# Threshold attention ahead of a two-layer network: transposed weights in the scores' spare PSUM columns, a new order of a period's instructions, and a small add moved to GpSimd

## The chip, the cores and the metric

The kernel runs on one core of a Trainium2 chip. The metric is the device time of one execution in microseconds (us); the lower the better. The core has five engines that matter here: TensorE (PE in the profile, with its weight loads as PEld), VectorE (DVE), ScalarE (ACT), GpSimd (POOL), and SyncE (SP), which issues the transfers. Each engine works through its own list of instructions in order, and waits at an instruction until the semaphores named in it have come.

## The reference, cut to what matters

```python
batch, n_heads, seq, head_dim = (8, 8, 576, 64)          # q, k, v: fp32
scores = (1 / sqrt(64)) * matmul(q, k.T)                 # per head: 576 x 576
thresh = max(scores, axis=-1) - tau                      # tau = 0.02
scores = where(scores >= thresh, scores, -1e9)
attn = exp(scores - max(scores))
attn = attn / (sum(attn) + 1e-9)
x = matmul(attn, v)  ->  (4608, 512)                     # heads side by side
h = maximum(x @ w_in, 0)                                 # w_in (512, 2048)
out = (h * h) @ w_out                                    # w_out (2048, 512)
```

The softmax has a threshold: of each row only the scores within tau of the row's maximum keep a weight, and the row is then divided by its sum plus 1e-9.

## The kernel before

The program has two stages. The attention comes first. The two layers of the network follow it, as products of blocks with sums of blocks formed ahead and after (a scheme that takes 49 block products where a plain one takes 64). The change touches only the attention.

Heads are taken two at a time: 32 pairs. The 576 query rows of a pair are four blocks of 128 and a rest of 64; the rests of two pairs make one more block. So there are 144 units of 128 rows by two heads, and `period(p)` handles two at once, A = 2p and B = 2p+1, over 72 periods, with a few more at both ends to fill and drain. The order of instructions is written out by hand in `period`: the order of the calls is the order on every engine, and the framework only adds the waits between engines.

The work of a unit, and where it runs:

- `scores_rest` (L373, or L376 for a shared rest) and `scores` (L386), on TensorE, write the scores of both heads into one tile `sc` of three PSUM banks, 1536 columns. Head 0 takes columns 0 to 575, head 1 takes 960 to 1535; columns 576 to 959, all in the middle bank, are spare (`SPARE`). There are two `sc` tiles, which fill six of the eight PSUM banks.
- `top` (L401, VectorE) finds the negative row maxima of both heads, `least` (L404, VectorE) the thresholds, `power` (L409, ScalarE) the exponentials of one head, `mask` (L414, VectorE) zeroes what lies under the threshold and sums the rows, `over` (L420, VectorE) adds 1e-9 to the two sums, `inverse` (L423, VectorE) takes reciprocals, and `normal` (L426, GpSimd) multiplies one head's weights by them.
- `fill` (L454, TensorE) transposes the weights, 9 blocks of 128x128 a unit and 18 for the two units of a period, into PSUM, and `filled` (L461, ScalarE) copies them to a tile `wT` in SBUF. These transposes go to the two PSUM banks that `bank` hands out in turn (`pY`), and six go into the two `pv` banks, behind the results there.
- `values` (L472, TensorE) multiplies them by v, two periods after the scores. Its results in the two `pv` banks are copied out together with the first six transposes of the next pair of units, and go to DRAM as x.

`turn` (L336, copied out in L339 or L341) transposes the queries or the keys of the next pair; `turn_last` (L351) does the rest of both, with its copies in L355 and L356 and two small GpSimd copies in L359. A table `TURNS` says which periods do it: of nine, four turn queries, four turn keys and one turns nothing.

The weights of the network are prepared beside the attention: `convert1` to `convert6` (L203 and L210 on ScalarE, L217 and L241 on GpSimd, L225 and L233 on VectorE) convert one of 32 pieces from 64-bit to 32-bit floats in each of 32 periods, and `sums_step` makes one of the 88 sums of weight blocks on GpSimd (L132 and L135), up to three in a period that converts nothing.

SyncE issues all loads and stores in one queue: queries (L291), keys (L305, L309), the rests (L310), values (L320), x (L518), weights (L183) and the finished weight sums (L521).

Of the kernel before, what the change touches and what calls it, by code (L numbers as in the profile page):

```python
# [48 lines left out]
def kernel(  # L49
# [236 lines left out]
    def load_q(i):  # L286
        b, hp = pairs[i]
        h = 2 * hp
        qn = sb.tile([P, FULL, P], FP32, tag="qn", name="qn")
        for j in range(2):  # L290
            nc.sync.dma_start(  # L291
                out=qn[:, :, ds(j * D, D)], in_=q[b, h + j, 0:MAIN, :].rearrange("(t p) d -> p t d", p=P)
            )
        loaded[i] = [qn]

    def load_k(i):
        b, hp = pairs[i]
        h = 2 * hp
        kn = sb.tile([P, FULL, P], FP32, tag="kn", name="kn")
        rn = sb.tile([P, P], FP32, tag="rn", name="rn")  # L300
        for j in range(2):
            queue = nc.scalar if i == 0 and j == 0 else nc.sync
            keys = k[b, h + j, :, :].rearrange("(p c) d -> p c d", c=CH)
            for e in range(2):
                queue.dma_start(  # L305
                    out=kn[ds(e * HALF, HALF), :, ds(j * D, D)],
                    in_=keys[:, j : j + CH - 1, :].rearrange("p (t e) d -> p t e d", e=2)[:, :, e, :],
                )
            queue.dma_start(out=rn[REST:P, ds(j * D, D)], in_=keys[:, 0 if j else CH - 1, :])  # L309
        nc.sync.dma_start(  # L310
            out=rn[0:REST, :].rearrange("p (j d) -> p j d", j=2),
            in_=q[b, h : h + 2, MAIN:S, :].rearrange("j p d -> p j d"),
        )
        loaded[i] += [kn, rn]

    def load_v(i):
        b, hp = pairs[i]
# [5 lines left out]
        )  # L323
        loaded_v[i] = va

    def turn(i, which):

        if which == 0:
            turned[i] = (
                sb.tile([P, MAIN], FP32, tag="qT", bufs=2, name="qT"),  # L330
                sb.tile([P, S], FP32, tag="kT", bufs=3, name="kT"),
            )
        nat, to = loaded[i][which], turned[i][which]
        pt = bank([P, FULL, P], "pqk")
        for t in range(FULL):
            nc.tensor.transpose(pt[:, t, :], nat[:, t, :], ident[:, :])  # L336
        flat, to = pt[:, :, :].rearrange("p t m -> p (t m)"), to[:, 0:MAIN]
        if which:
            nc.scalar.copy(to, flat)  # L339
        else:  # L340
            nc.scalar.activation(out=to, in_=flat, func=AF.Identity, scale=qscale[:, :])  # L341
            if i + 1 < len(pairs):
                load_q(i + 1)

    def last_q(i):
        return qdiag[i // 2 % 2][:, i % 2, :]

    def turn_last(i, pt):

        rn = loaded.pop(i)[2]  # L350
        nc.tensor.transpose(pt, rn[:, :], ident[:, :])  # L351

        def then():
            to = last_q(i)[:, ds(i % 2 * REST, REST)]
            nc.scalar.activation(out=to, in_=pt[:, 0:REST], func=AF.Identity, scale=qscale[:, :])  # L355
            nc.scalar.copy(turned[i][1][:, MAIN:S], pt[:, REST:P])  # L356
            for j in range(2):
                rows = ds(j * D, D)
                nc.gpsimd.tensor_copy(out=kdiag[i % 3][rows, ds(j * REST, REST)], in_=turned[i][1][rows, MAIN:S])  # L359
            if i + 1 < len(pairs):  # L360
                load_k(i + 1)

        return then

# [2 lines left out]
    def scores_rest(n, sc):  # L367
# [7 lines left out]
        for c, i in enumerate(pair):  # L375
            nc.tensor.matmul(to, last_q(i)[:, :], kdiag[i % 3][:, :], start=(c == 0), stop=(c == 1))  # L376

    def scores(n, sc):

        pair, t = units[n]  # L380
        for c in range(2):
            for j in range(2):
                rows, at = ds(j * D, D), ds(c * HALF, HALF)
                qT, kT = turned[pair[c]]
                lhs = qT[rows, ds(t * P + c * HALF, HALF)] if t < FULL else last_q(pair[c])[rows, at]
                nc.tensor.matmul(sc[at, ds(j * 2 * BANK, MAIN)], lhs, kT[rows, 0:MAIN], start=True, stop=True)  # L386

    AT = (0, 2 * BANK - REST)

    def softmax(n, sc):  # L390
# [26 lines left out]
            )  # L417

        def over():
            nc.vector.tensor_scalar(out=sm, in0=sm, scalar1=1e-9, scalar2=None, op0=ALU.add)  # L420

        def inverse():
            nc.vector.reciprocal(out=rs, in_=sm)  # L423
# [8 lines left out]
    def do(n, what, *args):  # L432
# [2 lines left out]

    wT = {}

    FILLS = (
        [(0, c) for c in range(3)], [(1, c) for c in range(3)],
        [(0, c) for c in range(3, 7)], [(1, c) for c in range(3, 7)],  # L440
        [(u, c) for c in (7, 8) for u in range(2)],
    )
    AT_OF = {
        uc: f * BANK + (P * (i + 1) if f < 2 else P * i) for f, fill in enumerate(FILLS) for i, uc in enumerate(fill)
    }

    def fill(m, f, pt):

        if has(2 * m):
            if m not in wT:  # L450
                wT[m] = sb.tile([P, 5 * BANK], FP32, tag="wT", bufs=1, name="wT")
            for i, (u, c) in enumerate(FILLS[f]):
                w = weights[2 * m + u]
                nc.tensor.transpose(pt[:, ds(P * (i + (f < 2)), P)], w[:, c, :, :].rearrange("p j d -> p (j d)"), ident[:, :])  # L454
        else:
            wT[m] = sb.tile([P, 5 * BANK], FP32, tag="wT", bufs=1, name="wT")

    def filled(m, f, pt, pv=False, copy=nc.scalar.copy):

        a, z = P if f < 2 and not pv else 0, BANK if has(2 * m) else P  # L460
        copy(wT[m][:, ds(f * BANK + a, z - a)], pt[:, a:z])  # L461

    def values(m):

# [2 lines left out]
        for c in range(CH):  # L467
            for u in range(2):
                for s, (i, _, count, row) in enumerate(halves(2 * m + u)):
                    for j in range(2):  # L470
                        rows = ds(j * D, D)
                        nc.tensor.matmul(  # L472
                            out[j][ds(u * D, D), ds(row, count)], loaded_v[i][rows, c, :],
                            x[rows, ds(AT_OF[u, c] + row, count)],
                            start=(c == 0 and s == 0), stop=(c == CH - 1), skip_group_check=True,
                        )
        return out
# [9 lines left out]
                    if i + 3 < len(pairs):  # L487
                        load_v(i + 3)

    def give_x(m, x):  # L490

        for u in range(2):
            rows = ds(u * D, D)
            for i, first, count, row in halves(2 * m + u):
                b, hp = pairs[i]
                to = xT[b][ds(hp * P, P), ds(first, count)].rearrange("(j d) n -> d j n", j=2)
                of = x[rows, 0 : 2 * BANK].rearrange("p (j n) -> p j n", j=2)[:, :, ds(row, count)]
                given.append((to, of))

    def has(n):  # L500
        return 0 <= n < NU
# [27 lines left out]
    def begun(n):  # L529
        return starts.get(n)  # L530

    TURNS = {}
    for g in range(2, 2 * len(pairs)):
        two, x = divmod(g - 4, 4)
        TURNS.setdefault(max(1, (9 * two + 5 + 2 * x) // 2), []).append(g)

    def period(p):

        A, B_, a, b = 2 * p, 2 * p + 1, 2 * p - 2, 2 * p - 1
# [13 lines left out]
                return pt  # L553

        def begin(n):
            if has(n):
                sc[n] = sc_pool.tile([P, 3 * BANK], FP32, tag="sc", name="sc")
                scores_rest(n, sc[n])

        do(a, "mask", 0)  # L560
        do(a, "mask", 1)
        do(a, "over")
        do(a, "inverse")
        do(a, "normal", 0)
        do(a, "normal", 1)
        begin(A)
        if has(A):
            scores(A, sc[A])
            softmax(A, sc[A])
        convert3(begun(p - 1))  # L570
        pt4 = other(m, 4)
        if pt4:
            filled(m, 4, pt4)
        for g in turns:
            turn(g // 2, g % 2)
        convert1(begun(p))
        convert2(begun(p))
        then = None
        begin(B_)
        if turns and turns[-1] % 2:  # L580
            then = turn_last(turns[-1] // 2, sc[B_][:, SPARE : SPARE + P])
        do(b, "mask", 0)
        do(b, "mask", 1)
        if has(B_):
            scores(B_, sc[B_])
            softmax(B_, sc[B_])
        do(A, "top")
        do(b, "over")
        do(b, "inverse")
        do(b, "normal", 0)  # L590
        do(b, "normal", 1)
        pv = values(m) if has(2 * m) else None
        do(A, "power", 0)
        do(A, "least")
        do(A, "power", 1)
        do(B_, "top")
        if then:
            then()
        pt0 = first(0, pv)
        pt1 = first(1, pv)  # L600
        do(B_, "power", 0)
        if pt0:
            filled(m + 1, 0, pt0, pv)
        if pt1:
            filled(m + 1, 1, pt1, pv)
        if pv:
            valued(m)
            give_x(m, wT[m + 1])
        do(B_, "power", 1)
        ask(False)  # L610
        convert4(begun(p - 1))
        do(B_, "least")
        convert5(begun(p - 1))
        sums_step()
        pt2 = other(m + 1, 2)
        if pt2:
            filled(m + 1, 2, pt2)
        pt3 = other(m + 1, 3)
        if pt3:
            filled(m + 1, 3, pt3)  # L620
        convert6(begun(p - 1))
        sums_start(p)
        if begun(p - 1) is None:
            sums_step()
        if begun(p - 1) is None:
            sums_step()
        fetch(begun(p + 2))
        ask(False)
# [304 lines left out]
    with tc.manual_schedule():  # L933
        with ExitStack() as stack:
# [15 lines left out]
            nc.scalar.activation(out=first[:, 0, :], in_=ident[:, 0:2], func=AF.Exp)  # L950
            load_v(0)
            keep_busy(10)
            turn(0, 0)
            turn(0, 1)
            turn_last(0, bank([P, P], "pqkr")[:, :])()
            for i in range(1, 3):
                load_v(i)
# [126 lines left out]
```

## Time and profile before

| | |
|---|---|
| three runs, median | 1408.46 us (1407.82 to 1408.79) |
| the profiled execution, its own time | 1406.65 us |
| its span, first to last instruction | 1404.9 us |
| clock of TensorE granted | 0.998 of full speed |
| first and last maximum (L401) | 12.0 and 591.0 us |
| first product of the two layers in the chain that ended last | 606.17 us |
| PE, DVE, ACT, POOL busy over the whole span | 96%, 76%, 61%, 67% |

The profile is one execution of the program. A row of the groups by line names the line of the kernel, the engine, the operation, the tiles written and read, the shapes and the count; then the total busy time in us and the mean of one in ns; then the idle time of that engine just before these instructions, and what ended most of it. A row of the timeline begins with the start in us and the duration of the merged instructions in us. Matmuls overlap and their ends are modelled, so TensorE's steps are best read from one start to the next. Nearly all tiles of the attention lie in one big tile, which the profile calls `arena`.

### The profile page before, as it was taken

The numbers are of one execution on the slowest core, as the hardware profiler recorded it, in microseconds if no ns is written. First come the engines' busy times: TensorE is split into PE (matmuls) and PEld (weight loads), VectorE is DVE, ScalarE is ACT, GpSimd is POOL, SyncE is SP. The second block draws the span as 40 slices with busy tenths as digits, with TensorE's granted clock in tenths as the row PEclk, the third lists the DMA queues.
The fourth block names the chain that finished last, engine by engine and source line by source line (L and its number), as shares of the span: only waits on it lengthen the run. The fifth ranks groups of instructions, "written<-read, shape, count | busy, mean of one in ns | idle before, by whom it ended". The sixth has DMA issues, their size and how long they took to land.

```text
span 1404.9 us, 40543 instructions
## 1 busy us (share of the span) xinstructions
PE 1351.1 (96%) x15882; PEld 1188.3 (85%) x15882; DVE 1070.6 (76%) x2280; ACT 850.6 (61%) x1579; POOL 943.8 (67%) x967
## 2 busy tenths in 40 slices
PE   7999999899999999999999999999999999999998
PEld 4676666666666767699999999999999999999998
DVE  5999999999999998857787778877765456654563
ACT  5888777688887777737665667656643233332330
POOL 2666788867778885335665566555887777777775
PEclk9999999999999999999999999999999999999999
DMA  4554326785432222123323433237962444224411
GB/s 113 130 138 129 81 56 187 208 262 156 123 100 64 72 64 68 29 69 131 114 105 111 144 128 113 103 110 282 396 208 87 147 150 144 67 96 147 151 32 31
DMA packets 205295, 177.24 MB, mean 126 GB/s; under 512 B 96304, under 2 KB 149552, under 8 KB 205104
## 3 DMA queue, kind: packets, MB, share of 16 engines
q1 hardware_dynamic: 203792, 174.24, 40.2%
q8 instruction: 125, 2.05, 0.6%
q14 instruction: 66, 0.54, 0.1%
q10 hardware_dynamic: 1312, 0.41, 0.1%
HBM read 105.12 MB, written 69.47 MB: 124 GB/s over the span
## 4 chain that ended last, share of the span: by engine, by line
PE 53%; DVE 1%; POOL 1%; ACT 1%; issue 0%; DMA 0%; DVEq 0%; POOLq 0%
PE po L891 28%; PE ph L756 25%; DVE arena L135 1%; POOL arena L135 1%; ACT arena L670 0%; ACT arena L735 0%; DMA w<-w 0%; DVEq L135 0%; POOLq L135 0%; ACT arena L736 0%
## 5 line engine op out<-in xcount | busy, mean ns | idle before, releaser
L135 POOL TENSOR_TENSOR arena<-arena 128x512 f32<-128x512 f32 (+1 forms) x314 | 376.4, 1220 | 252.4 <-DVE arena L135 213.7
L756 PE MATMUL ph<-arena,w 128*128 128x128 f32 x3528 | 396.6, 275 | 1.9 <-DVE arena L135 0.8
L756 PEld LDWEIGHTS ph<-arena,w 128*128 128x128 f32 x3528 | 394.7, 192 | 3.8 <-DVE arena L135 3.1
L891 PE MATMUL po<-w,arena 128*128 128x128 f32 x3528 | 396.6, 275 | 0.3
L891 PEld LDWEIGHTS po<-w,arena 128*128 128x128 f32 x3528 | 394.8, 192 | 2.0 <-issue 1.6
L135 DVE TENSOR_TENSOR arena<-ph,arena 128x512 f32<-128x512 f32 x378 | 255.7, 689 | 94.1 <-PE ph L756 63.4
L426 POOL TENSOR_SCALAR arena<-arena 128x576 f32<-128x576 f32 x288 | 211.2, 747 | 130.3 <-DVE arena L404 65.0
L135 DVE TENSOR_TENSOR arena<-po,arena 128x128 f32<-128x128 f32 x378 | 108.2, 290 | 169.4 <-PE po L891 165.8
L414 DVE SCALAR_TENSOR_TENSOR arena<-sc,arena 128x576 f32<-128x576 f32 x288 | 222.9, 811 | 11.8 <-ACT arena L409 11.2
L409 ACT ACTIVATE arena<-sc,arena 128x576 f32<-128x576 f32 x288 | 206.4, 752 | 28.1 <-DVE arena L401 20.4
L401 DVE TENSOR_REDUCE arena<-sc 128x2 f32<-128x1152 f32 x144 | 195.2, 1355 | 26.7 <-PE sc L386 25.9
L702 ACT COPY c<-arena 128x512 f32<-128x512 f32 (+1 forms) x303 | 172.9, 579 | 63.0 <-DVE arena L132 55.8
L472 PEld LDWEIGHTS pv<-arena 64*64 64x64 f32 x5760 | 154.9, 133 | 36.9 <-issue 21.6
L454 PEld LDWEIGHTS pY<-ident,arena 128*128 128x128 f32 x864 | 90.4, 140 | 112.6 <-ACT arena L461 104.4
L132 DVE TENSOR_TENSOR arena<-arena,c 128x512 f32<-128x512 f32 (+1 forms) x267 | 175.0, 664 | 7.8 <-ACT c L702 6.9
L132 POOL TENSOR_TENSOR arena<-arena 128x512 f32<-128x512 f32 (+1 forms) x138 | 174.3, 1263 | 9.7
L461 ACT COPY arena<-pY 128x512 f32<-128x512 f32 x216 | 120.7, 604 | 79.8 <-PE pY L454 79.8
L454 PE MATMUL pY<-ident,arena 128*128 128x128 f32 x864 | 129.9, 286 | 32.9 <-ACT arena L461 32.9
L386 PE MATMUL sc<-arena 64*64 64x512 f32 x1152 | 159.4, 624 | 0.0
L472 PE MATMUL pv<-arena 64*64 64x128 f32 (+1 forms) x5760 | 157.8, 259 | 0.7 <-ACT arena L461 0.7
L735 ACT ACTIVATE arena<-arena 128x512 f32<-128x512 f32 x144 | 89.9, 624 | 77.2 <-POOL arena L135 77.0
L670 ACT COPY arena<-po 128x128 f32<-128x128 f32 x63 | 16.7, 265 | 178.9 <-PE po L891 177.1
(56 smaller groups left out, 1047.2 us busy)
## 6 DMA issues: line engine op xcount, KB each, us to landing
g<-arena SPq DMA_DIRECT2D x144, 256.0 KB, 2.0
arena<-g SPq DMA_DIRECT2D x144, 256.0 KB, 4.7
w<-w SPq DMA_DIRECT2D x98, 256.0 KB, 5.1
arena<-in_v_dram SPq DMA_DIRECT2D x32, 288.0 KB, 3.3
out_dram<-arena SPq DMA_DIRECT2D x70, 128.0 KB, 2.2
arena<-in_q_dram SPq DMA_DIRECT2D x64, 128.0 KB, 3.3
arena<-in_moe_w_out_dram SPq DMA_DIRECT2D x16, 512.0 KB, 4.0
xT<-arena SPq DMA_DIRECT2D x128, 64.0 KB, 2.1
```

The source lines that it names most:

```text
L132: e.tensor_tensor(out=out, in0=x, in1=y, op=ALU.subtract)
L135: e.tensor_tensor(out=out, in0=x, in1=y, op=ALU.add)
L386: nc.tensor.matmul(sc[at, ds(j * 2 * BANK, MAIN)], lhs, kT[rows, 0:MAIN], start=True, stop=True)
L401: nc.vector.tensor_reduce(out=nmx, in_=both, axis=AXIS.X, op=ALU.max, negate=True)
L409: nc.scalar.activation(out=w[:, :, j, :], in_=of(j), func=AF.Exp, bias=nmx[:, j : j + 1], scale=1.0)
L414: nc.vector.scalar_tensor_tensor(out=w[:, :, j, :], in0=of(j), scalar=thr[:, j : j + 1], in1=w[:, :, j, :], op0=ALU.is_ge, op1=ALU.mult, a ...
L426: nc.gpsimd.tensor_scalar(out=w[:, :, j, :], in0=w[:, :, j, :], scalar1=rs[:, j : j + 1], scalar2=1.0, op0=ALU.mult, op1=ALU.mult)
L454: nc.tensor.transpose(pt[:, ds(P * (i + (f < 2)), P)], w[:, c, :, :].rearrange("p j d -> p (j d)"), ident[:, :])
L472: nc.tensor.matmul(out[j][ds(u * D, D), ds(row, count)], loaded_v[i][rows, c, :], x[rows, ds(AT_OF[u, c] + row, count)], start=(c == 0 and ...
L702: nc.scalar.copy(c, y)
L756: nc.tensor.matmul(to[:, j, :], W_IN[m, k][:, ts(j, P)], of[k][:, m - 1, :], start=(not more and j == 0), stop=True, skip_group_check=True,)
L891: nc.tensor.matmul(to, g[:, j, :], w[:, j, :], start=(not more and j == 0), stop=(j == 3), skip_group_check=True)
```

## The change

The 18 transposes of a period are divided anew, in six portions of 1, 3, 3, 4, 4 and 3 (in periods that turn keys 2, 3, 3, 4, 3 and 3). The first two go into the `pv` banks as before, two go into `pY` banks, and the other two, six transposes, go into the spare columns of the `sc` tiles of A and B, between `scores_rest` and `scores`. `apart` tells the framework that the copies of the spare columns and the main scores touch different banks, so that neither has to wait for the other. The tile of the last turn moves from the spare columns to the end of a `pY` bank.

The order in `period` is new. The masks of A now follow in the same period, so `over`, `inverse` and `normal` of A come half a period later than its masks; the masks of B stay at the start of the next period. `over` runs on GpSimd. The steps of the weight conversion and the weight sums are placed anew, and in periods that turn keys and convert nothing, two sums are made in place of three. Keys are loaded as soon as both the keys and the rests of the pair before have been transposed.

```diff
+        def then():
+            if which:
+                nc.scalar.copy(to, flat)
+                next_keys(i)
...
         def over():
-            nc.vector.tensor_scalar(out=sm, in0=sm, scalar1=1e-9, scalar2=None, op0=ALU.add)
+            nc.gpsimd.tensor_scalar(out=sm, in0=sm, scalar1=1e-9, scalar2=None, op0=ALU.add)
...
+            sizes = (2, 3, 3, 4, 3, 3) if turned_last(m + 2) else (1, 3, 3, 4, 4, 3)
+            order = [(u, c) for u in range(2) for c in range(CH)]
...
+        def spare(m, f, n):
+            if has(2 * m):
+                pt = sc[n][:, SPARE : SPARE + 3 * P]
+                fill(m, f, pt)
+                return pt
+
+        pt3 = other(m, 4)
+        then = None
+        if turned_last(p):
+            at = pt3 if pt3 else bank([P, BANK], "pL")
+            then = turn_last(turns[-1] // 2, at[:, 3 * P : 4 * P])
         begin(A)
+        do(b, "mask", 0)
+        convert3(begun(p - 1))
+        do(b, "mask", 1)
+        ptA = spare(m, 2, A)
         if has(A):
             scores(A, sc[A])
             softmax(A, sc[A])
+        if pt3:
+            filled(m, 4, pt3)
+        if then:
+            then()
+        last = [turn(g // 2, g % 2) for g in turns]
+        if ptA is not None:
+            aside(A, filled(m, 2, ptA))
         convert1(begun(p))
+        pt2 = other(m, 3)
+        do(a, "inverse")
+        do(b, "over")
+        do(A, "top")
+        convert4(begun(p - 1))
         begin(B_)
+        ptB = spare(m, 5, B_)
+        do(a, "normal", 1)
+        for done in last:
+            done()
+        if pt2:
+            filled(m, 3, pt2)
+        do(A, "least")
+        if ptB is not None:
+            aside(B_, filled(m, 5, ptB))
+        do(A, "power", 0)
+        do(a, "normal", 0)
         if has(B_):
             scores(B_, sc[B_])
             softmax(B_, sc[B_])
         do(b, "inverse")
+        do(B_, "top")
+        do(A, "power", 1)
+        do(A, "mask", 0)
+        do(A, "mask", 1)
+        convert2(begun(p))
         pv = values(m) if has(2 * m) else None
+        do(b, "normal", 1)
+        do(B_, "least")
         pt0 = first(0, pv)
         pt1 = first(1, pv)
+        do(b, "normal", 0)
         do(B_, "power", 0)
+        sums_step()
         if pt0:
             filled(m + 1, 0, pt0, pv)
+        convert5(begun(p - 1))
+        do(A, "over")
+        do(B_, "power", 1)
         if pt1:
             filled(m + 1, 1, pt1, pv)
...
-        if begun(p - 1) is None:
+        if begun(p - 1) is None and not turned_last(p):
             sums_step()
```

## The prediction

> **What bounds the kernel now.** I read the page first, for the shares, and then the busy time by stretch, because the page averages an attention stage (to about 606 us) with the two layers behind it, which the change does not touch. Columns: start:end, length, then busy us and instructions of each engine, the clock, the DMA share and rate.
>
> ```profile
> 50.00:100.00 50.00, 47.49 (x776) 34.07 (x776) 46.71 (x115) 43.19 (x81) 31.17 (x45) 1.00 0.48 123
> 300.00:350.00 50.00, 46.87 (x728) 32.73 (x721) 49.15 (x109) 42.03 (x78) 36.86 (x48) 1.00 0.66 185
> 500.00:550.00 50.00, 47.49 (x775) 34.11 (x775) 45.23 (x101) 37.24 (x67) 36.61 (x44) 1.00 0.29 73
> ```
>
> TensorE and VectorE are both near full, so the shares alone do not name the bound. The groups by line do better: what each engine idled for.
>
> ```profile
> L454 PEld LDWEIGHTS pY<-ident,arena 128*128 128x128 f32 x864 | 90.4, 140 | 112.6 <-ACT arena L461 104.4
> L454 PE MATMUL pY<-ident,arena 128*128 128x128 f32 x864 | 129.9, 286 | 32.9 <-ACT arena L461 32.9
> L461 ACT COPY arena<-pY 128x512 f32<-128x512 f32 x216 | 120.7, 604 | 79.8 <-PE pY L454 79.8
> L414 DVE SCALAR_TENSOR_TENSOR arena<-sc,arena 128x576 f32<-128x576 f32 x288 | 222.9, 811 | 11.8 <-ACT arena L409 11.2
> L420 DVE TENSOR_SCALAR arena<-arena 128x2 f32<-128x2 f32 x144 | 55.4, 385 | 2.5
> L426 POOL TENSOR_SCALAR arena<-arena 128x576 f32<-128x576 f32 x288 | 211.2, 747 | 130.3 <-DVE arena L404 65.0
> ```
>
> TensorE's transposes into `pY` wait for ScalarE to copy the previous bank out, and ScalarE waits for those transposes: two banks handed to and fro. VectorE spends 55 us on 144 adds of 128x2. The timeline of one period shows both (TensorE's rows, two copies, one add):
>
> ```profile
> 302.31 1.15 PE L454 MATMUL pY<-ident,arena 128*128 128x128 f32 x8 [0.39 <-ACT arena L461]
> 303.10 1.27 POOL L132 TENSOR_TENSOR arena<-arena 128x512 f32<-128x512 f32 x1
> 303.14 1.25 DVE L420 TENSOR_SCALAR arena<-arena 128x2 f32<-128x2 f32 x1
> 303.30 0.42 PE L373 MATMUL sc<-arena 128*128 128x128 f32 x2
> 303.64 1.09 PE L386 MATMUL sc<-arena 64*64 64x512 f32 x8
> 304.67 0.66 PE L454 MATMUL pY<-ident,arena 128*128 128x128 f32 x4
> 305.16 0.60 PE L336 MATMUL pqk<-ident,arena 128*128 128x128 f32 x4
> 306.11 0.49 PE L373 MATMUL sc<-arena 128*128 128x128 f32 x2 [0.36 <-DVE arena L414]
> 306.53 1.09 PE L386 MATMUL sc<-arena 64*64 64x512 f32 x8
> 307.44 2.15 PE L472 MATMUL pv<-arena 64*64 64x128 f32 x72
> 309.52 0.87 PE L454 MATMUL pv<-ident,arena 128*128 128x128 f32 x6
> 310.14 1.07 ACT L461 COPY arena<-pv 128x512 f32<-128x512 f32 x2 [0.26 <-PE pv L454]
> 310.78 1.14 PE L454 MATMUL pY<-ident,arena 128*128 128x128 f32 x8 [0.39 <-ACT arena L461]
> ```
>
> Start to start this period is 8.47 us: 0.99 + 0.34 + 1.03 + 0.49 + 0.95 + 0.42 + 0.91 + 2.08 + 1.26. Most of TensorE's steps repeat to within 0.01 us. The six `pv` transposes are worth 0.67 (0.112 each: line 756 makes 3528 in 396.6 us), so 0.59 of the 1.26 is a wait for the first `pv` copy, every period. The 0.95 holds 0.51 of wait for a mask (0.44 elsewhere, for example in periods without the 1.25 us add). So before is a TensorE chain of matmuls plus fixed bank waits, with VectorE's stalls on top. VectorE is not the bound by itself: its steps start to start (reduction 1.27, mask 0.74, small ones 0.1 to 0.2) sum to 6.4 us, 7.3 in a period with weight conversion, unstalled.
>
> The mean period is 8.13 us: the reductions (line 401) start from 12.0 to 591.0 us, the last being a second unit, 1.9 us behind its first, so 577.1/71.
>
> **The change, part by part.** V is the start of the value products (L472).
>
> *Transposes.* The 18 stay 18, at 0.112. Before: 6 into `pv`, then 8 and 4 into `pY`. After: 4 or 5 into `pv` (1 or 2, then 3), 3 or 4 into `pY` first thing in the next period, 3 into spare columns between a unit's remainder scores and its main scores, 4 into `pY`, 3 into the second unit's spare columns. The spare ones wait for no bank copy, and the listing of the changed instructions gives the main scores no wait on ScalarE. What remains: the first `pY` transposes still need the bank of the first `pv` tile.
> That wait, from the rows: first copy starts 0.62 after the first transpose (three of 0.112, 0.28 of handing over), lasts 0.60, TensorE goes on 0.04 later. After, with one transpose and a copy of 256 columns: 604 ns for 512 and 500 for 384 (the copy out of `pX`) give about 0.40, so 0.11 + 0.28 + 0.40 + 0.04 = 0.83. With two transposes and 384 columns: 1.04.
>
> *TensorE's period after* (a turn of queries): 2.08 values, 0.83, first `pY` 0.49, remainder 0.34, spare 0.34, scores 0.91, `pqk` 0.44, `pY` 0.49, 0.34, 0.34, 0.91 = 7.51. A turn of keys: 7.72. No turn: 7.07. In nine periods there are four, four and one: 7.55. Before, without stalls, the same steps give 7.88 (queries), 8.08 (keys, 0.2 for the remainder's transpose between the scores) and 7.44: 7.92. The shared remainder unit adds 0.08 to both. So 8.00 becomes 7.63: 0.37 x 72 = 27 us.
>
> *The add.* 55.4 us leave VectorE; only the part that others waited for counts. The measured 8.13 is 0.13 above 8.00, about 9 us of such stalls. On GpSimd the add is in no row; bounds 0.10 (128x1 memset) to 0.75 (the 128x576 multiply); I take 0.23, the 64x64 copy of line 359, nearest in size. Twice per period that is 0.5 us of GpSimd, busy 37 of 50 us. Queued behind the second unit's add are its own and the first unit's multiplies; the reciprocal waits for it on VectorE, ahead of the second reduction. In a period with three weight sums: first unit's masks end V+3.0, add 3.25, two sums of 1.28 5.8, second add 6.05; the reciprocal is reached about V+7.1. It fits. GpSimd's whole load is 4 x 0.75 + 3 x 1.28 + 0.5 = 7.3, just inside 7.6; in periods that turn keys one sum is dropped, which pays for the two 64x64 copies and makes the 44 input-weight sums end some three periods later (about the 66th of 72), covered by the attention still running.
>
> *The shared port.* The add's row reads 155/169/1256 ns (min, median, max), and each long one ends 23 to 30 ns after a GpSimd instruction's end. The Trainium skill (SBUF — State Buffer, section "Who interferes with whom") says the same as a rule, and it speaks against this order: a VectorE tensor_scalar on SBUF is locked out for a whole GpSimd instruction. The threshold (line 404) and the shift (line 225) are such instructions, and now stand where GpSimd multiplies. Before, the trace charged line 404 only 51 ns a time over its median (262 against 211), 7 us in all. By the rule a threshold arriving at random in a 0.75 us multiply loses 0.37, so 27 us of VectorE over 72 periods. VectorE's slack before the second reduction is about 0.5 us (first reduction from V-2.2, then threshold and reciprocal to V-0.3, scores ready at V+0.25), so in plain periods I cost it at nothing. In the 32 conversion periods the shift (0.43) uses the slack up; there I charge 0.2: 6 us.
>
> *Waits added.* The first reduction now waits also for ScalarE's copy of the spare columns (seen in the listing). ScalarE reaches that copy at about V+5.0 behind the first `pY` copy and two small ones; it ends at 5.4, where the scores are ready at 5.2 in a key period: 0.2 into the same slack. Six copies replace five: about 0.19 us each of fixed cost (604 less 4 x 104), 13 us of ScalarE, which is busy 37 to 43 of 50; the cover is thinnest in conversion periods, and is in the 6 us above.
>
> *Moved at no cost.* Both masks of the first unit come a half period earlier; that frees its slot sooner, and the second slot's remainder scores need the mask at about V+5.2 and are reached at 5.8. Key loads are issued after the keys' turn instead of at the period's end, query loads unchanged in order: earlier by some us against a need 2.25 periods (17 us) later, landing 3.3 us. SP keeps its 1,013 rows; x's stores stay behind the `pv` copies. If the cover fails, one late key load stalls TensorE by its landing, 3 us, once. The clock is 1.00 throughout.
>
> Sum: -27 - 9 + 6 = -30 us. The profiled execution was 1406.65 (span 1404.9 and 1.75 around it), so 1377; the median shown is 1.8 higher: **1378**. Working ranges: the `pv` wait 0.1 either way (7 us), the stalls 0 to 15.
>
> **Rivals.**
> A, the copy is late anyway: ScalarE has to do the second unit's first exponential before the first `pv` copy. That needs the second reduction (V+0.25 + 1.39) and so is done at V+2.3 against transposes ready at 2.5. If VectorE's port stalls or the new ScalarE wait delay the reduction by over 0.2, every microsecond passes on to TensorE. With 0.3 lost in all periods, 1378 + 22 = 1400. For: conversion periods have no slack left. Against: before had the same order there and waited a steady 0.39 + 0.2.
> B, the wait vanishes: TensorE's floor without it is 7.63 - 0.44 = 7.19; 0.94 x 72 = 68 us, 1341. Against: the first `pY` still names that bank.
> C, slower: GpSimd's add blocks VectorE. The reciprocal stands ahead of the second reduction, and the second add behind sums, conversion and copies. In the walk it has 1.1 us to spare and VectorE 0.5 behind that; from 2.1 us late in every period (1.6 of cover, 0.5 of gain) the change loses. At 2.6 late: +0.5 x 72, 1444. It takes an add near 0.75 twice, plus a sum waiting for VectorE's port. Against: half of the periods carry no three sums, and GpSimd idled 130 us before these multiplies.
> D, the change doesn't do what it says: the tracker could serialise scores behind the spare copies. The listing shows no such wait; then about 1407.
>
> **How the numbers follow.** About 0.2% (2.8 us) is what a measurement of this kernel can tell from no change. The main case, 1364 to 1392: 0.64. A, 1392 to 1405: 0.17. B: 0.07. C: 0.09. D and sums that cancel: 0.03. Faster 0.88, same 0.03, slower 0.09. The range 1362 to 1399 leaves out B, C, D and the worst of A, some 2 in 10.
>
> **What would show it.** Right: mean distance of first reductions near 7.7 us; `pv` to `pY` at 0.83 and 1.04 in place of 1.26; ScalarE releasing spare transposes nowhere; the add on GpSimd near 0.2 us; the layers behind start near 576 us instead of 606 and last as long. Wrong: reciprocals that idle for GpSimd, a first reduction ended by ScalarE's copy, thresholds of 0.4 us and more on the path, or a `pv` step still at 1.2.

## The result and the profile after

| | before | after |
|---|---|---|
| median, same chip | 1408.14 us (1406.34 to 1408.79) | 1385.32 us (1383.25 to 1388.32) |
| profiled execution | 1406.65 us | 1383.25 us |
| first to last unit maximum | 12.0 to 591.05 us | 11.8 to 569.6 us |
| mean period (72 first maxima, 71 distances) | 8.13 us | 7.82 us |

The ratio is 0.9842, with a 95% interval of 0.9817 to 0.9867: faster by 23 us, where 30 were forecast. The gain is made in the attention: the first maxima of the periods span 577.1 us before and 555.4 after, 21.7 less. The two layers behind it start at 583.1 us where they started at 606.2 (576 was forecast), and last as long as before (798.3 us, before 798.7).

Busy time by stretch, after, in the same three stretches (start:end, length, then PE, PEld, DVE, ACT, POOL, the clock, the DMA share, GB/s):

```profile
50.00:100.00 50.00, 48.06 (x790) 34.26 (x792) 49.55 (x104) 46.09 (x91) 38.40 (x60) 1.00 0.52 137
300.00:350.00 50.00, 46.63 (x773) 33.54 (x775) 46.72 (x105) 45.10 (x89) 45.22 (x65) 1.00 0.70 201
500.00:550.00 50.00, 48.06 (x809) 34.83 (x801) 40.74 (x88) 38.98 (x77) 36.57 (x56) 1.00 0.25 60
```

Each stretch holds more of TensorE's instructions than before, and GpSimd has gone from 37 to 45 us in the middle one. VectorE has not become the bound: from 500 us on it is busy 41 of 50. In the first stretch it is busy 49.55 of 50, and still does not set the pace: the periods there take 7.45 to 7.85 us, no more than later. The groups by line, after, for the lines that the prediction read (the last row is VectorE's reduction in the kernel before):

```profile
L499 PEld LDWEIGHTS pY<-ident,arena 128*128 128x128 f32 x546 | 60.0, 140 | 51.9 <-issue 25.3 <-POOL w L132 8.7 <-ACT arena L505 8.4
L499 PE MATMUL pY<-ident,arena 128*128 128x128 f32 x546 | 85.9, 278 | 28.3 <-ACT arena L505 24.8 <-POOL arena L453 2.5 <-POOL w L132 0.9
L499 PE MATMUL sc<-ident,arena 128*128 128x128 f32 x432 | 70.8, 273 | 0.2 <-ACT arena L505 0.2
L428 DVE TENSOR_REDUCE arena<-sc 128x2 f32<-128x1152 f32 x144 | 195.1, 1355 | 53.5 <-PE sc L411 49.2 <-ACT arena L505 1.5 <-issue 0.3
L447 POOL TENSOR_SCALAR arena<-arena 128x2 f32<-128x2 f32 x144 | 47.5, 330 | 83.9 <-DVE arena L441 46.1 <-DVE arena L450 16.3 <-DVE arena L431 14.5
L453 POOL TENSOR_SCALAR arena<-arena 128x576 f32<-128x576 f32 x288 | 213.9, 757 | 19.0 <-DVE arena L450 11.2 <-PE sc L411 1.0
L450 DVE RECIPROCAL arena<-arena 128x2 f32<-128x2 f32 x144 | 22.6, 157 | 2.1 <-POOL arena L447 2.1
L401 DVE TENSOR_REDUCE arena<-sc 128x2 f32<-128x1152 f32 x144 | 195.2, 1355 | 26.7 <-PE sc L386 25.9
```

The third row is the change's core: 432 transposes into spare columns of `sc` idle 0.2 us in all. Those into `pY` still wait 24.8 us for ScalarE. VectorE now waits longer for TensorE ahead of its reductions (49.2 us, before 25.9), as an engine with time to spare does. The reciprocals wait for GpSimd's add 2.1 us in all. GpSimd's own idle time ahead of its multiplies fell from 130 to 19 us; 83.9 us of idle time now lie ahead of its adds.

One period that turns keys, after (timeline: start, duration; TensorE's rows, two copies and a reduction):

```profile
454.17 2.15 PE L516 MATMUL pv<-arena 64*64 64x128 f32 x72
454.49 1.36 DVE L428 TENSOR_REDUCE arena<-sc 128x2 f32<-128x1152 f32 x1 [0.88 <-PE sc L411]
456.25 0.77 PE L499 MATMUL pv<-ident,arena 128*128 128x128 f32 x5
456.77 0.48 ACT L505 COPY arena<-pv 128x384 f32<-128x384 f32 x1
457.39 0.52 PE L499 MATMUL pY<-ident,arena 128*128 128x128 f32 x3 [0.38 <-ACT arena L505]
457.75 0.27 PE L365 MATMUL pY<-ident,arena 128*128 128x128 f32 x1
457.78 0.59 ACT L505 COPY arena<-pv 128x512 f32<-128x512 f32 x1
457.86 0.39 PE L386 MATMUL sc<-arena 128*128 128x128 f32 x2
458.08 0.49 PE L499 MATMUL sc<-ident,arena 128*128 128x128 f32 x3
458.50 1.09 PE L411 MATMUL sc<-arena 64*64 64x512 f32 x8
459.52 0.66 PE L345 MATMUL pqk<-ident,arena 128*128 128x128 f32 x4
460.01 0.60 PE L499 MATMUL pY<-ident,arena 128*128 128x128 f32 x4
460.45 0.39 PE L386 MATMUL sc<-arena 128*128 128x128 f32 x2
460.67 0.49 PE L499 MATMUL sc<-ident,arena 128*128 128x128 f32 x3
461.09 1.09 PE L411 MATMUL sc<-arena 64*64 64x512 f32 x8
462.00 2.15 PE L516 MATMUL pv<-arena 64*64 64x128 f32 x72
```

It takes 7.83 us where 7.72 were worked out. The three spare transposes cost 0.42 and 0.42, start to start, and nothing holds them. Taken as medians over the attention, the steps that were forecast came out so:

| step, start to start, us | forecast | after | before |
|---|---|---|---|
| `pv` (4) to first `pY` | 0.83 | 0.926 | 1.267 (6) |
| `pv` (5) to first `pY` | 1.04 | 1.142 | |
| first `pY` (4) to remainder | 0.49 | 0.465 | 0.983 (8) |
| remainder + spare transposes | 0.34 + 0.34 | 0.223 + 0.421 | |
| main scores to `pqk` | 0.91 | 1.020 | 1.020 (to `pY`) |
| main scores to values | 0.91 | 0.909 | 0.909 |
| sum, queries / keys / no turn | 7.51 / 7.72 / 7.07 | 7.61 / 7.83 / 7.12 | 7.82 / 7.93 / 7.39 |

From about the 40th period on, after repeats one pattern of nine periods to 0.01 us (7.83 7.84 7.83 7.75 7.83 7.84 7.83 7.61 7.34), where before scattered between 7.4 and 9.1. What is left outside the pattern are a few periods in the middle: the 30th takes 10.26 us, the 35th to 37th take 8.75, 8.60 and 8.48.

The theory that the experiments start from: the gain has two parts of about equal size, shorter steps on TensorE (fewer waits for bank copies) and stalls of VectorE that the new order and the moved add take away. The rivals: the add alone does it; the order alone does it and the spare columns only bring extra copies; or GpSimd is now so full that it sets the end.

### The profile page after: what moved, and what is told of

Same layout as the page of the kernel before. It is cut to its first block, busy times and chain, and to the rows that moved or that the text cites. A ratio compares the mean times of both kernels' runs of the same rounds, so it can differ in the third digit from the quotient of the medians.

```text
span 1381.5 us, 40859 instructions
## 1 busy us (share of the span) xinstructions
PE 1339.5 (97%) x15882; PEld 1180.6 (85%) x15882; DVE 1025.5 (74%) x2136; ACT 860.5 (62%) x1651; POOL 990.1 (72%) x1111
## 5 line engine op out<-in xcount | busy, mean ns | idle before, releaser
L428 DVE TENSOR_REDUCE arena<-sc 128x2 f32<-128x1152 f32 x144 | 195.1, 1355 | 53.5 <-PE sc L411 49.2
L516 PEld LDWEIGHTS pv<-arena 64*64 64x64 f32 x5760 | 151.6, 133 | 40.1 <-issue 21.7
L499 PE MATMUL pY<-ident,arena 128*128 128x128 f32 x546 | 85.9, 278 | 28.3 <-ACT arena L505 24.8
L447 POOL TENSOR_SCALAR arena<-arena 128x2 f32<-128x2 f32 x144 | 47.5, 330 | 83.9 <-DVE arena L441 46.1
L499 PEld LDWEIGHTS pY<-ident,arena 128*128 128x128 f32 x546 | 60.0, 140 | 51.9 <-issue 25.3
```

The lines of the kernel that those rows point to most:

```text
L428: nc.vector.tensor_reduce(out=nmx, in_=both, axis=AXIS.X, op=ALU.max, negate=True)
L499: nc.tensor.transpose(to, w[:, c, :, :].rearrange("p j d -> p (j d)"), ident[:, :])
L516: nc.tensor.matmul(out[j][ds(u * D, D), ds(row, count)], loaded_v[i][rows, c, :], x[rows, ds(plans[m].at[u, c] + row, count)], start=(c == ...
```

## Experiments

**The add back on VectorE.**

```diff
-            nc.gpsimd.tensor_scalar(out=sm, in0=sm, scalar1=1e-9, scalar2=None, op0=ALU.add)
+            nc.vector.tensor_scalar(out=sm, in0=sm, scalar1=1e-9, scalar2=None, op0=ALU.add)
```

> The changed kernel with one line undone: the add of 1e-9 runs on VectorE again, in the new order. Theory 1 (the gain is TensorE's shorter bank waits; VectorE now idles about 0.9 us ahead of the second reduction of a period, so a stalled add is covered): 1383 to 1392 us, at most 6 us over the changed kernel's 1385, periods of 7.83 us unchanged where no weight sums run. Theory 2 (the gain is mostly the add taken off VectorE, 55 us busy and up to 1.25 us each behind a GpSimd sum): most of the 23 us go, 1398 to 1408 us.

Measured: 1392.12 us, ratio 0.9886 (0.9868 to 0.9904), 7 above after. The line's own view (durations are min/median/max in ns):

```profile
L447 DVE TENSOR_SCALAR arena<-arena x144: 152/169/1319, 17.6 to 583.5; 128x2 f32<-128x2 f32 x144
  POOL arena L453: 58.1, 31
```

The second line is who waited: GpSimd's multiplies, 58.1 us in 31 cases. The cost lies only where GpSimd makes sums: the mean period is 8.18 in periods 19 to 34 (numbered as the program's `p`, from 0; 7.89 after) and 7.92 in 50 to 65 (7.73 after), and 8.22 in 35 to 45 (7.94 after), which convert a piece and make one or two sums each; periods without sums are the same (2 to 15: 7.78 and 7.77). So in the new order the add's move is worth 7 of the 23 us, and the add alone does not carry the change.

**The add alone, in the kernel before.**

```diff
-            nc.vector.tensor_scalar(out=sm, in0=sm, scalar1=1e-9, scalar2=None, op0=ALU.add)
+            nc.gpsimd.tensor_scalar(out=sm, in0=sm, scalar1=1e-9, scalar2=None, op0=ALU.add)
```

> The kernel before with one line changed: the add runs on GpSimd, the old order kept, so the reciprocal stands right behind it on VectorE and waits for GpSimd's queue. Theory 1: no gain, and slower where weight sums are queued ahead of the add: 1405 to 1440 us. Theory 2: most of the gain comes with this line alone: 1385 to 1398 us. The recorded rival C (an add late on GpSimd blocks VectorE) shows here if anywhere: reciprocals that idle for the add by 0.5 to 2 us.

Measured: 1449.02 us, ratio 1.0288 (1.027 to 1.0305): 40 us slower than before. The waits (who <- for whom: us, times, longest) and the add's row say why:

```profile
DVE arena L423 <- POOL arena L420: 94.7, 73, 3.7
L420 POOL TENSOR_SCALAR arena<-arena x144: 213/213/221, 17.1 to 640.4; 128x2 f32<-128x2 f32 x144
```

The add itself takes 213 ns every time, but it stands behind sums of 1.28 us, and in the old order the reciprocal needs it at once: VectorE stands 94.7 us. Periods with sums take 9.27 and 9.37 (periods 19 to 34, and 50 to 65), those without 7.98 and 7.83 (2 to 15, and the last six), as before. This is the mechanism of the prediction's rival C, in the order where it belongs; that its price comes close (1444) is chance, since it was worked out for the new order. The same edit costs 40 us in one order and brings 7 in the other.

**The new order without the spare columns.** The six transposes go to a bank of the two that are handed in turn, and the copy of a turn is called earlier, so that its bank comes free.

```diff
-                pt = sc[n][:, SPARE : SPARE + 3 * P]
+                pt = bank([P, BANK], "pS")
...
+        for done in last:
+            done()
         begin(B_)
         ptB = spare(m, 5, B_)
         do(a, "normal", 1)
-        for done in last:
-            done()
```

> The changed kernel without the spare columns: both portions of three transposes take a bank in turn as the others do, and the turn's copy is called before the second portion so that its bank comes free. Theory 1: two more hand-overs of a bank per period, of which 0.3 to 0.8 us are not covered: 1405 to 1440 us. Rival (order and add make the gain, the columns none): 1383 to 1392 us.

Measured: 1423.3 us, ratio 1.0107 (1.0091 to 1.0123): 38 us above after, and slower than before. Groups by line, and the place in one period:

```profile
L499 PEld LDWEIGHTS pS<-ident,arena 128*128 128x128 f32 x432 | 45.3, 140 | 39.6 <-ACT arena L505 23.4 <-ACT arena L353 9.9 <-ACT arena L350 5.1
460.61 0.39 PE L386 MATMUL sc<-arena 128*128 128x128 f32 x2
461.17 0.55 PE L499 MATMUL pS<-ident,arena 128*128 128x128 f32 x3 [0.18 <-ACT arena L505]
461.65 1.09 PE L411 MATMUL sc<-arena 64*64 64x512 f32 x8
```

The step from remainder to transposes is 0.56 (median) in place of 0.22, the next 0.48 in place of 0.42, twice a period, and most regular periods take 8.24 to 8.56. Four portions of transposes a period now queue for the two banks, where the kernel before had three; the new order pays only with the spare columns. The reverse, spare columns in the old order, was not run.

**The deal of the blocks.** The `pv` step was 0.10 longer than worked out. After, the first `pY` transposes take blocks of the second unit, whose last weights GpSimd has just multiplied, so they wait for GpSimd as well as for ScalarE's copy. Here the portions are dealt so that these transposes take earlier blocks; their sizes stay.

```diff
-            self.fills = [order[sum(sizes[0:f]) : sum(sizes[0 : f + 1])] for f in range(6)]
+            self.fills, k = [None] * 6, 0
+            for f in (0, 1, 4, 3, 2, 5):
+                self.fills[f] = order[k : k + sizes[f]]
+                k += sizes[f]
```

> The changed kernel with the 18 blocks dealt out in another order: the first pY portion of a period holds blocks of the first unit, whose multiplies TensorE has already waited for, so its first transpose waits for ScalarE alone and no longer for ScalarE and GpSimd; the GpSimd wait moves to the spare portion behind it. Sizes, engines and copies are the same. The step from pv to pY measured 0.926 and 1.142 us where 0.83 and 1.04 were worked out; the copy ends 0.14 us before TensorE goes on, 0.04 in the kernel before. If the second wait costs this 0.10: 0.10 x 72 = 7 us less, 1376 to 1380 us. If the hand-over is the copy's own: no change, 1383 to 1388 us.

Measured: 1381.72 us, ratio 0.9807 (0.979 to 0.9824). That is 4 us below after, where 7 were expected of this cause and none without it. The `pv` steps are 0.835 and 1.051, where 0.83 and 1.04 had been worked out; in after they were 0.10 longer in nearly every period alike, which speaks against weights that came late. The line views of the transposes, after and here, show what went (an EVENT_SEMAPHORE is a wait that stands ahead of the instruction as one of its own; 51 ns each):

```profile
L499 PEldq EVENT_SEMAPHORE  x103: 51/51/51, 21.9 to 577.6; - x103
```

```profile
L502 PEldq EVENT_SEMAPHORE  x33: 51/51/51, 21.0 to 576.2; - x33
```

Before has 2 of them. The Trainium skill (Perfetto Trace Analysis, section "Identifying Dependency Chains") says that an instruction that waits for several engines may get such instructions ahead of it. Here 70 fewer go with 0.09 us less at each of 71 hand-overs. The regular pattern falls by 0.06 a period, not 0.09: the step behind, from the first `pY` transposes on, is 0.03 longer in every period (0.383 for 0.355 in turns of keys, 0.492 for 0.465 in the others). Why is open.

**The same two on another chip.**

> The changed kernel as it is, as the yardstick for the other three on the same chip: 1383 to 1388 us.

> The kernel with the other order of blocks again, against the changed kernel on the same chip. Its first run showed steps of 0.835 and 1.051 us from pv to pY against 0.926 and 1.142, so 0.091 in each period; the periods that hold a turn got 0.06 shorter. 72 x 0.06 to 0.09: 4 to 6.5 us under the changed kernel.

Measured: 1385.26 (ratio 0.9833, 0.9819 to 0.9847) and 1382.14 (0.9811, 0.9798 to 0.9825): 3.1 us apart, under what was expected. The pattern is faster by 0.063 x 72 = 4.5 us. In the two profiles irregular periods shift the difference both ways: the 30th takes 12.71 us here and 11.15 in the kernel after, the second 7.68 here and 9.77 there, with the clock of TensorE at half for 3.4 us.

**Three sums in every period that converts nothing.**

```diff
-        if begun(p - 1) is None and not turned_last(p):
+        if begun(p - 1) is None:
```

> The changed kernel with three weight sums again in the periods that turn keys and convert nothing (13 of the 30 periods with sums), so GpSimd has 1.28 us more work there, ahead of the second unit's add. Recorded rival C says that a late add holds the reciprocal and with it the second reduction. By my walk GpSimd would be at 7.3 + 0.55 (two 64x64 copies) = 7.9 us of work in a period of 7.8, so the add comes up to 1 us late, of which VectorE's idle 0.9 covers most: 0 to +0.5 us in those periods, 0 to 7 us in all, 1384 to 1392. If GpSimd had room to spare: no change in time. If each sum went straight onto the path: 13 x 1.28 = +17 us.

Measured: 1387.7 us, ratio 0.9855 (0.9841 to 0.9869). Busy time from 430 to 500 us, after and then here:

```profile
430.00:500.00 70.00, 67.15 (x1108) 48.47 (x1110) 58.38 (x128) 54.11 (x108) 60.88 (x86) 1.00 0.29 70
```

```profile
430.00:500.00 70.00, 67.08 (x1105) 48.26 (x1103) 59.49 (x127) 54.31 (x107) 65.67 (x90) 1.00 0.29 70
```

GpSimd is busy 65.67 of 70 us and the periods are the same to 0.01. So GpSimd does not set the end, and the sum that the change drops need not be dropped for its sake. The 2.4 us over the kernel after are within the two intervals, and in the profile they lie in two periods of the middle (the 35th takes 9.37; the 39th takes 12.50, with a hole of 2.9 us in TensorE's work and the clock at half for 6.8 us behind it).

**The order of the transfers.** Next to the dealt blocks: x is stored first, then values and the weight piece are loaded, and the weight sums are stored last.

```diff
         if pv:
+            give_x(m, wT[m + 1], plans[m + 1].size[0])
+        while given:
+            to, from_ = given.popleft()
+            nc.sync.dma_start(out=to, in_=from_)
+        if pv:
             valued(m)
-            give_x(m, wT[m + 1], plans[m + 1].size[0])
+        convert6(begun(p - 1))
+        fetch(begun(p + 2))
         ask(False)
-        convert6(begun(p - 1))
...
-        fetch(begun(p + 2))
```

> The kernel with the other order of blocks, and with the issues on SyncE in another order at a period's end: x's stores first, then the value loads, the weight load, and only then the finished weight sums. In the changed kernel one period took 10.27 us, where the pv copy waited 2.52 us for x's store behind 576 KB of value loads, and three took 8.5 to 8.8, where ScalarE waited up to 1.8 us for a weight piece. If the order of issue is the cause: these four shrink by 2 to 4 us in all, 1376 to 1380. If the transfers' total is the cause (260 GB/s there): as the kernel with the other order of blocks, 1380 to 1382.

Measured: 1383.58 us, ratio 0.9829 (0.9813 to 0.9845), no better than the dealt blocks alone. The copy's wait for x's store in the 30th period was 1.8 us, against 2.3 and 3.2 in the two profiles of the dealt blocks, but the period still took 10.82 (there 10.02 and 12.71), and the irregular ones only moved (the 40th takes 9.98). That fits a queue that is already behind from the period ahead, which an order inside one period does not mend.

**Fewer stores of weight sums at a time.** Next to the dealt blocks, at each of the two places of a period one store is issued where there were up to two.

```diff
-        for _ in range(len(later) if every else min(2, len(later))):
+        for _ in range(len(later) if every else min(1, len(later))):
```

> The kernel with the other order of blocks, and at most one finished weight sum stored at each of the two places of a period, in place of two; every sum is still stored, later. In the profiles so far the steady nine periods repeat to 0.01 us, and what lies above them is one period of 10 to 12.7 us where the pv copy waits for x's store (while stores of weight sums of 256 KB are in flight) and three to five of 8.4 to 8.9 where ScalarE waits for a weight piece. If the stores' rate causes these waits: 3 to 5 us less than that kernel's 1382, so 1377 to 1379. If not, or if they only move to later periods: 1380 to 1384.

Measured: 1377.49 us (1377.37 to 1381.26), ratio 0.9788 (0.9772 to 0.9804): the fastest version, better than before and after. Its interval lies clear of after's, and overlaps those of the dealt blocks alone. The time is what was expected, but the traces speak for another reason. SyncE's issues and ScalarE's copy in the 30th period, after:

```profile
229.81 2.85 SPq L565 DMA_DIRECT2D w<-w  x3
232.71 2.23 SPq L740 DMA_DIRECT2D arena<-xT  x4
240.43 1.02 SPq L320 DMA_DIRECT2D arena<-in_v_dram  x2
241.55 1.91 SPq L562 DMA_DIRECT2D xT<-arena  x3
244.92 0.48 ACT L505 COPY arena<-pv 128x384 f32<-128x384 f32 x1 [2.52 <-DMA xT<-arena]
```

and with fewer stores:

```profile
227.79 2.01 SPq L568 DMA_DIRECT2D w<-w  x2
238.74 1.91 SPq L565 DMA_DIRECT2D xT<-arena  x3
242.07 0.48 ACT L508 COPY arena<-pv 128x384 f32<-128x384 f32 x1 [1.86 <-DMA xT<-arena]
```

From the first issue of x's stores to the copy that overwrites their source it is 3.37 us in the one and 3.33 in the other: the transfer is not faster. It is issued 0.6 earlier against the work (1.03 us ahead of the `pv` transposes, where it was 0.42), and the wait is 0.66 shorter; two stores of sums stand ahead of it on SyncE where there were three. The dealt blocks' two profiles follow the same sum: issued 0.70 ahead, the wait was 2.33; issued 0.24 behind, it was 3.15. SyncE had issued in the kernel after without a pause for 13 us there, 18 transfers at some 0.7 us each, with seven loads of keys and rests and four for the layers (L740) among them; whether the earlier key loads of the change put them there was not run. So in this period the wait goes with the length of SyncE's queue, not with the rate of the transfers as I had put it. The kernel before had the same wait in about the same place (1.95 us for x's store, at 253 us).

Not all of the gain is the stores'. Against the dealt blocks' first profile the first maxima span 4.5 us less: 2.2 of that lies in the first two periods, where the clock of TensorE was at half for 10.2 us there and 3.4 here, 0.5 in the 30th period and 1.9 in the 34th to 40th.

## Why the prediction was right or wrong

*Sign, range and the main mechanism were right.* The spare transposes wait for nothing, the first `pY` still waits for its bank, and 1385.3 lies between 1362 and 1399. The size was 30 forecast and 23 measured; that it came so close is in part luck, because two of its terms missed in opposite directions.

*Transposes, 27 us forecast, 12 measured: the term that was mis-sized.* By the medians of the steps the period falls from 7.90 to 7.74, with the shared unit's 0.08 in both: 0.16 x 72 = 12. Three errors of about 0.1 us a period, less a fourth in the other direction, make up the difference of 0.21.
- I took 0.91 for main scores to `pqk`, reading the 1.020 of before as a wait for the bank. In the timeline above the last copy that frees that bank ends by 458.37, ahead of the scores at 458.50, and the step is 1.02 all the same. What both cases share is that 64x64 products are followed by 128x128 ones; no run isolates that. It cost about 0.11.
- The `pv` step had 0.10 more than worked out, from a second wait; the deal of the blocks took away 0.09 of it and left 0.835 and 1.051.
- I read before's steps 0.10 too high (7.92 without the shared unit, by its medians 7.82): 0.06 in every period from steps of one period that lie above the median, 0.34 for 0.317 at the remainders above all, and 0.04 on average from 0.2 for a remainder's transpose that is worth 0.11.
- The other way, the remainders with their spare transposes took 0.07 less than forecast, and the first `pY` 0.03 less.

*Stalls, 9 us forecast to go, 16 there.* With steps of 7.90, before's 8.13 held 0.23 a period. In the new order the add on VectorE costs 7; how before's 16 divide between the add and the order, no run tells.

*New stalls, 6 us forecast, about 6 found, for another reason, so that this agreement is luck.* After's 7.82 is 0.08 to 0.09 above its steps. I had charged conversion periods for VectorE locked out behind GpSimd. The rule of the Trainium skill that I weighed (SBUF — State Buffer, "Who interferes with whom") agrees with the trace but did not cost time: the thresholds read 209/226/973 ns (min, median, max) and took 16 us over their median, before 7 (the 40 longest each end 21 to 26 ns behind a GpSimd instruction), the shifts read 416/440/834, and the time is in VectorE's slack (L428 above). The conversion periods 2 to 15 take 7.77 on average, where the regular pattern has 7.74. What costs are transfers: the 30th period's x store (2.5 us), and ScalarE waiting for weight pieces in the 35th to 37th (3.8 us in 5 cases).

So 12 + 16 - 6 = 22, beside 21.7 measured. The three terms are differences of the same measured periods, so that they close says nothing for the split; it rests on the steps' medians.

*Rivals.* A did not come: the `pv` copies start as soon as their transposes are there (456.77 above). B did not: the wait of 0.38 stands. C did not come in the new order (2.1 us), and did, at 40 us, in the old one. D did not.

## What to carry to other kernels

Spare columns of a PSUM tile are worth using when they take work out of a hand-over between two engines, and not for the space: here the kernel took 38 us more when the same six transposes queued for shared banks. Move a small operation to another engine only with its consumer moved away from it, since what it costs is the queue that it stands in (213 ns of work, up to 3.7 us of waiting), and count the semaphores at a hand-over: the second one cost 0.09 us each time here. When the chain is tight and repeats, look at the few periods that do not, and there at the issuing queue before the transfers.

## What the hardware showed that was not expected

A hole of two to three and a half us in TensorE's work can halve its clock for a while, in some executions. In the 30th period of the dealt blocks' second profile TensorE stood from 241.1 to 244.5 us; of the order of transfers, from 241.6 to 243.6. Windows of the two, and then one of the kernel after and of its second profile (same columns as above, the clock third from the end):

```profile
242.00:243.00 1.00, 0.00 (x0) 0.00 (x0) 0.00 (x0) 0.00 (x0) 1.00 (x1) 1.00 0.91 304
243.00:250.00 7.00, 5.51 (x24) 3.57 (x25) 2.93 (x6) 3.21 (x8) 3.49 (x7) 0.51 0.88 263
```

```profile
243.00:244.00 1.00, 0.41 (x4) 0.41 (x5) 0.00 (x0) 0.94 (x2) 0.92 (x2) 1.00 1.03 288
244.00:248.00 4.00, 4.00 (x22) 2.06 (x21) 2.33 (x6) 1.83 (x6) 3.06 (x6) 0.57 1.01 345
```

```profile
240.00:255.00 15.00, 11.92 (x214) 8.98 (x206) 10.72 (x23) 10.21 (x21) 11.28 (x16) 1.00 0.76 233
```

```profile
240.00:255.00 15.00, 12.47 (x190) 8.70 (x192) 8.79 (x18) 9.03 (x18) 11.22 (x16) 0.89 0.76 232
```

At half speed 0.51 over 7 us is 6.9 us, 0.57 over 4 us is 3.4 us, and 0.89 over 15 us is 3.3 us. The kernel after had a hole of 2.8 us in its own profile and kept 1.00; in its second profile it had one of 2.5 and did not. The Trainium skill (TensorE: Matmul & The Clock Gate, Part 1) has the clock halved after an idle window of about 3.4 us, with windows that run freely; the length of the slow stretches agrees, but here a hole of 2.0 us was enough. So one late store, for which the copy waited 3.15 us, could cost 5 (12.71 against a regular 7.77). It may also be a part of why runs of one kernel lie some 4 us apart: the four runs of after had clocks of 1.000 and 0.998 at 1383.3, 0.997 and 0.995 at 1387.3 and 1388.3, and with fewer stores all five had 0.998 or 0.999. That is not shown: these are means over an execution, which do not tell where the slow stretches lay, and the dealt blocks had 0.996 at 1381.8 beside 0.999 at 1382.0.
